# Batch 0's keys and queries: three adjacent tokens a partition in two halves, instead of two tokens a partition in three blocks

## The chip, the cores and the metric

The kernel runs on one core of a Trainium2 chip. A core has five engines with queues of their own (TensorE for matmuls, VectorE, ScalarE, GpSimd, and SyncE, which here issues most of the DMAs) and 16 DMA engines, which move data between the chip's memory and the core's on-chip buffers. Matmul results go into PSUM, in banks of 512 fp32 columns on 128 partitions; all else lies in SBUF. The metric is the time of one execution on the device, in microseconds (us), as the median of several runs.

## What is computed

Attention over 4 batches, 8 heads, 768 tokens and 64 numbers a head, with a window of fewer than 16 tokens to either side, and beside it one summary for each block of 32 tokens (the maximum of its keys, the mean of its values). Then a Fourier mix over tokens and channels, a normalization and two dense layers. Cut to what matters:

```python
k_sum = k.reshape(B, H, nb, 32, D).max(axis=3)
v_sum = v.reshape(B, H, nb, 32, D).mean(axis=3)
scores_l = scale * q @ k.T                      # kept where |i - j| < 16
scores_s = scale * q @ k_sum.T + log(32)
a = softmax(concatenate([scores_l, scores_s]))
x = a @ concatenate([v, v_sum])                 # then heads side by side: (B, 768, 512)
u = x + real(fft(fft(x, axis=1), axis=2))
out = u + maximum(layernorm(u) @ w_ch1, 0) @ w_ch2
```

All arithmetic is fp32; the weights come as float64 and are converted on the chip.

## The kernel before

Heads are taken in pairs: a group `g` holds heads 2g and 2g + 1, so a batch has four groups. Batch 0 is computed first and alone, by `first_attention`. For VectorE and TensorE its instructions stand in the order in which they are written (`tc.manual_schedule`), and SP issues the DMAs of that part in written order too (`fetch` pins them). For the rest the order on each engine is chosen when the program is built. The attention of the later batches is spread between the dense layers of the batch before.

For a group of batch 0 the steps are these.

- `load(b, g)` fetches the keys (`kn`) and the queries (`qn`), 384 KB each, into tiles with the tag `nat`, of which there are four. A partition p holds, for each of two heads `e` and of three blocks `j` of 256 tokens, the tokens 256 j + 2 p and 256 j + 2 p + 1. They lie next to each other in memory, so each run of bytes is 2 x 64 x 4 = 512 bytes.
- `prepare(b, g)` turns them so that the 64 numbers of a head lie along the partitions (two heads fill 128) and the tokens along the columns. It does so with matmuls against the identity: the loaded data are the stationary operand, `ident` the moving one. As a partition has every second token of its block, TensorE writes the columns `s`, `s + 2`, `s + 4`, ... of the bank (L700). The two heads go to the two halves of the partitions. ScalarE copies the banks to `kt` (keys, with 16 columns of padding at either end) or to `qt` (queries): one bank of 512 columns and one of 256 (L702). Then VectorE takes the maximum of each block of 32 keys into `km` (L715).
- `wide_scores(b, g)` multiplies keys and queries in stretches of 64 queries against 96 keys (L731) and against the block maxima (L735), for one half of the tokens (384) and then for the other. The first half of the queries is all that the first half of the scores needs of `qt`. ScalarE takes exponentials (L737), VectorE applies the band (`wide`).
- `wide_values(b, g)` multiplies by the values in `vw` (L758) and divides (L762 and after it).

At the start of the program, SP issues the loads of the keys and queries of group 0, of the keys of group 1, of a batch's values for the block means (`words`, 768 KB in rows of 8192 bytes), of the queries of group 1, and of the values in bands (`vw`). ScalarE issues five small tables: `ident`, `wide` (twice: the band and the counts), `sel` and `half`. L1468 is a VectorE instruction that multiplies `half` by 32; the text has it behind the first attention, and on VectorE it stands ahead of the first `km`. A pair of matmuls on a small tile (`warm`, L1414) runs on TensorE before the first data are there.

In the trace each fp32 matmul leaves two records, so the 12 matmuls that turn one tensor count as x24.

Of the kernel before, what the change touches and what calls it, by code (L numbers as in the profile page):

```python
# [16 lines left out]
P = 128  # L17
# [473 lines left out]
def _main_program(ctx, tc, q, k, v, moe_w_ch1, moe_w_ch2, out):  # L491


    nc = tc.nc
    B, H, S, D = q.shape
# [10 lines left out]
    S2 = S // 2  # L506
    F2 = S // 4
    HT = NST // 2
# [17 lines left out]
    ident = cpool.tile([P, P], FP, name="ident")  # L526
# [24 lines left out]
    def fetch(out, in_):  # L551

        ins = nc.sync.dma_start(out=out, in_=in_)
        if in_order[0]:
            tc.keep_in_program_order(ins)

    def abank(shape, name):
        return psum.tile(shape, FP, tag="attn", bufs=4, name=name)

    def bank(shape, name):  # L560
        return psum.tile(shape, FP, tag="bank", bufs=4, name=name)
# [10 lines left out]
    nat, marks = {}, {}  # L572

    def load(b, g, *which):

        for n in which or (1, 0):
            t = nat[b, g, n] = apool.tile([P, 2, NST // 2, 2 * D], FP, tag="nat", bufs=4, name=f"{'qk'[n]}n_{b}_{g}")
            if (b, g) > (2, 0):
                t = nat[b, g, n] = t.rearrange("p e j n -> p (e j n)").rearrange("p (m c) -> p m c", c=32)
                for e in range(2):  # L580
                    for h in range(2):
                        r, o = D * e + 32 * h, (q, k)[n][b, 2 * g + e].offset + 32 * h
                        fetch(out=t[r:r + 32], in_=bass.AP((q, k)[n].tensor, o, [[D, 32], [32 * D, S // 32], [1, 32]]))
                continue
            fetch(out=t.rearrange("p e j n -> p (e j) n"),
                  in_=(q, k)[n][b, 2 * g:2 * g + 2].rearrange("e (j p s) d -> p (e j) (s d)", p=P, s=2))

# [55 lines left out]
    is_wide = lambda b: b == 0  # L643
# [39 lines left out]
    def prepare(b, g, *which):  # L683
        qn, kn = (nat[b, g, n] for n in range(2))
        kt, km = kt_bufs[g % 2], km_bufs[g % 2]
        qt = apool.tile([P, S], FP, tag="qt", name=f"qt_{b}_{g}") if 0 in (which or (0,)) else None
        for n in which or (1, 0):
            src, dst = (kn, kt[:, W:W + S]) if n else (qn, qt)
            if (b, g) > (2, 0):
                with tc.issue_after(marks["dense"]):  # L690
                    nc.vector.transpose(out=dst, in_=src.rearrange("p m c -> p (m c)"))
                continue
            if is_wide(b):
                for j0, j1 in ((0, 2), (2, 3)):
                    n = 2 * P * (j1 - j0)
                    ps = bank([P, n], f"qk_{b}_{g}_{j0}")
                    for j in range(j0, j1):
                        for s in range(2):
                            for e in range(2):
                                nc.tensor.matmul(ps[D * e:D * (e + 1), 2 * P * (j - j0) + s:2 * P * (j - j0 + 1):2],  # L700
                                                 src[:, e, j, D * s:D * (s + 1)], ident, start=True, stop=True)
                    nc.scalar.copy(out=dst[:, 2 * P * j0:2 * P * j1], in_=ps)  # L702
            else:
                for e in range(2):

                    ps = abank([P, S2], f"qk_{b}_{g}_{e}")
                    for j in range(NST // 2):
                        nc.tensor.transpose(ps[:, P * j:P * (j + 1)], src[:, e, j, :], ident)
                    for s in range(2):
                        nc.scalar.copy(out=dst[D * e:D * (e + 1), s:S:2], in_=ps[D * s:D * (s + 1)])  # L710
        if which == (0,):
            nat[b, g] = qt
            return
        with tc.issue_after(marks["fold", 0]) if (b, g) == (1, 0) else ExitStack():
            nc.vector.tensor_reduce(out=km[:, 0:nb], in_=kt[:, W:W + S].rearrange("p (n f) -> p n f", f=BLOCK),  # L715
                                    op=ALU.max, axis=AX.X)
        nat[b, g] = qt
# [110 lines left out]
    def first_attention():  # L828
# [3 lines left out]
        wt["fold"] = split_fold(0, fold)  # L832
        p = {0: wide_scores(0, 0, lambda: add_blocks(0))}
        prepare(0, 1)
        sum_values(0, 0)
        load(0, 3)
        for g in range(NP - 1):
            p[g + 1] = wide_scores(0, g + 1, (lambda: add_blocks(1)) if g == 1 else None)
            wide_values(0, g, p[g], x)
            load_values(*following(0, g, 2))  # L840
            for par in range(2):
                fold_sequence(par, g)
            if g == 0:
                get_tables(0)
            if g < NP - 2:
                prepare(0, g + 2)
                sum_values(0, g + 1)
            if g == NP - 3:
                load_raw(1)
                load(1, 0)  # L850
                load_raw(2)
                sum_values(0, g + 2)
# [105 lines left out]
    def gen_attention(b):  # L958
# [3 lines left out]
        if b == 2:  # L962
            load(2, 1)
            load(2, 2)
# [4 lines left out]
        for g in range(NP + 1):  # L969
# [36 lines left out]
            if n1:  # L1006
                prepare(*n1, *((1,) if b > 1 else ()))
# [404 lines left out]
    ps = bank([P, 512], "warm")  # L1412
# [19 lines left out]
    for vw in vw_bufs:  # L1432
        nc.gpsimd.tensor_copy(out=vw[:, :, D].rearrange("p (e n) -> p e n", e=2),
                              in_=count[:, None, :].to_broadcast([P, 2, NQ]))
# [47 lines left out]
    for b in range(B):  # L1482
# [14 lines left out]
        if b == B - 2:  # L1497
# [9 lines left out]
            ps = bank([1, 1], "flag_ps")  # L1507
# [42 lines left out]
```

## Time and profile before

| | us |
|---|---|
| median of 3 runs | 804.05 |
| lowest and highest of them | 803.28, 805.3 |
| profiled execution | 800.91 |
| its span, first to last instruction | 799.1 |
| TensorE busy in the span | 775.9 |
| VectorE, ScalarE busy | 496.6, 224.5 |

The profiled execution is one execution with the hardware profiler on; its span leaves out 1.8 us around the first and last instruction. The granted clock of TensorE was 0.993 of full speed over the span, and 0.66 between 10 and 20 us. In that stretch TensorE worked 7.25 us of 10; in the one before it 8.00.

How to read the profile: a busy engine isn't always at its peak, since matmuls overlap. A row of the timeline gives the start, the length, the engine, the line, the operation, what it writes and reads, and in brackets how long the engine had been idle before it and what it waited for. A name as `sc<-qt,kt` is output and inputs. DMA engines were busy to 86% over the first 10 us and over 100% in the next 20 (their packets overlap).

### The profile page before, as it was taken

To read this page: it belongs to the slowest core of one execution; us is meant where nothing else is said; L and a number is where in the kernel's file an instruction comes from. 1 tells how busy PE (TensorE), PEld (TensorE's weight loads), DVE (VectorE), ACT (ScalarE), POOL (GpSimd) and SP (SyncE) were. 2 spreads that over 40 slices of the span, in tenths; PEclk is the share of its full clock that TensorE was granted. 3 is DMA by queue.
4 is the path that set the end of the run, shared out by engine and by line. 5 is a ranking of instruction groups with operands and counts; after the bars stand their busy time and mean duration, and the time that the engine had idled before them with its cause. 6 is when DMAs were issued, how large, how long until landed. Compare 5 with 4: busy or idle time off the path is not lost.

```text
span 799.1 us, 14452 instructions
## 1 busy us (share of the span) xinstructions
PE 775.9 (97%) x5914; PEld 566.1 (71%) x5914; DVE 496.6 (62%) x1131; ACT 224.5 (28%) x493; POOL 52.0 (7%) x91
## 2 busy tenths in 40 slices
PE   7979899999999999999999999999999999999997
PEld 4768665445589866688578876688569875786686
DVE  3798998985997647562668634554576622533352
ACT  2544866533735121100136012100126102001200
POOL 0010000000000320000210510000120000000000
PEclk8999999999999999999999999999999999999999
DMA  9999797978755469946343459501614153106001
GB/s 212 227 193 200 174 311 237 250 206 265 222 142 160 129 196 266 166 70 163 128 164 120 132 210 173 132 2 54 232 55 139 53 196 139 61 0 231 0 28 55
DMA packets 135258, 121.83 MB, mean 152 GB/s; under 512 B 94448, under 2 KB 116688, under 8 KB 134992
## 3 DMA queue, kind: packets, MB, share of 16 engines
q1 hardware_dynamic: 133920, 118.53, 54.0%
q0 software_dynamic: 576, 2.10, 0.8%
q8 instruction: 48, 0.79, 0.4%
q10 hardware_dynamic: 688, 0.20, 0.1%
q14 instruction: 26, 0.21, 0.1%
HBM read 97.22 MB, written 23.59 MB: 151 GB/s over the span
## 4 chain that ended last, share of the span: by engine, by line
PE 84%; DVE 12%; DMA 2%; issue 1%; ACT 1%; ACTq 0%; SPq 0%; DVEq 0%
PE hx L1307 19%; PE ox L1376 17%; PE hz L1307 9%; PE oz L1376 9%; PE o L1353 5%; PE hy L1307 5%; PE oy L1376 4%; PE y L1203 3%; PE mx L1162 2%; PE sc L774 2%; DVE x L566 2%; DMA half<-c_half 1%; PE av L812 1%; PE av L807 1%; DVE u L566 1%; DVE w L566 1%
## 5 line engine op out<-in xcount | busy, mean ns | idle before, releaser
L1307 PE MATMUL hx<-u,w 128*128 128x384 f32 x512 | 185.8, 490 | 0.3 <-DVE h L566 0.3
L1307 PEld LDWEIGHTS hx<-u,w 128*128 128x128 f32 x512 | 95.1, 190 | 67.5 <-ACT p L780 2.5
L1307 PE MATMUL hz<-u,w 128*128 128x384 f32 x256 | 93.1, 486 | 0.0
L1376 PE MATMUL ox<-w,s 128*128 128x256 f32 x336 | 80.3, 380 | 0.9 <-DVE x L566 0.9
L1376 PE MATMUL oz<-w,s 128*128 128x256 f32 x336 | 80.7, 379 | 0.0
L1376 PE MATMUL ox<-w,h 128*128 128x256 f32 x336 | 79.6, 381 | 0.0
L566 DVE TENSOR_TENSOR x<-ox,x 128x256 f32<-128x256 f32 x84 | 35.2, 422 | 65.2 <-PE ox L1376 64.9
L1307 PEld LDWEIGHTS hz<-u,w 128*128 128x128 f32 x256 | 48.6, 190 | 34.2 <-ACT h L1326 0.5
L1376 PEld LDWEIGHTS ox<-w,h 128*128 128x128 f32 x336 | 62.9, 190 | 11.2 <-issue 1.2
L1318 ACT COPY h<-hx 128x384 f32<-128x384 f32 x32 | 15.3, 479 | 195.7 <-PE hx L1307 195.7
L1376 PEld LDWEIGHTS ox<-w,s 128*128 128x128 f32 x336 | 63.1, 190 | 10.1 <-DVE x L566 1.6
L1376 PEld LDWEIGHTS oz<-w,s 128*128 128x128 f32 x336 | 63.5, 190 | 8.5
L566 DVE TENSOR_TENSOR h<-hx,h 128x384 f32<-128x384 f32 x32 | 17.8, 556 | 51.2 <-PE hx L1307 51.2
L566 DVE TENSOR_TENSOR h<-hy,h 128x384 f32<-128x384 f32 x32 | 17.8, 557 | 49.1 <-PE hy L1307 49.0
L1307 PE MATMUL hy<-u,w 128*128 128x384 f32 x128 | 46.6, 487 | 0.0
L1353 PE MATMUL o<-w,h 128*128 128x512 f32 x96 | 41.9, 594 | 0.0
L1337 ACT ACTIVATE h<-hx 128x384 f32<-128x384 f32 x32 | 15.7, 491 | 87.2 <-PE hx L1307 87.1
L1376 PE MATMUL oy<-w,h 128*128 128x256 f32 x168 | 39.9, 379 | 0.0
L566 DVE TENSOR_TENSOR x<-oz,x 128x256 f32<-128x256 f32 x42 | 17.8, 423 | 31.1 <-PE oz L1376 30.8
L1307 PEld LDWEIGHTS hy<-u,w 128*128 128x128 f32 x128 | 24.2, 190 | 16.6 <-DVE h L566 0.2
L1376 PEld LDWEIGHTS oy<-w,h 128*128 128x128 f32 x168 | 31.9, 190 | 4.3
L1353 PEld LDWEIGHTS o<-w,h 128*128 128x128 f32 x96 | 18.0, 190 | 22.3 <-issue 21.7
(164 smaller groups left out, 1091.2 us busy)
## 6 DMA issues: line engine op xcount, KB each, us to landing
w<-dw SPq DMA_DIRECT2D x44, 896.0 KB, 5.6
words<-in_moe_w_ch_dram SPq DMA_DIRECT2D x32, 512.0 KB, 5.9
dw<-w SPq DMA_DIRECT2D x12, 896.0 KB, 6.1
vw<-in_v_dram SPq DMA_DIRECT2D x47, 192.0 KB, 5.5
out_dram<-x SPq DMA_DIRECT2D x24, 256.0 KB, 2.3
vb<-in_v_dram SPq DMA_DIRECT2D x24, 192.0 KB, 3.6
kn<-in_k_dram SPq DMA_DIRECT2D x9, 384.0 KB, 5.8
qn<-in_q_dram SPq DMA_DIRECT2D x9, 384.0 KB, 6.6
```

Source lines behind the costliest of these rows:

```text
L566: return nc.vector.tensor_tensor(out=out, in0=in0, in1=in1, op=op).ins
L774: nc.tensor.matmul(ps[h][r:r + 64, i, :], kt[rows, o:o + 64], qt[rows, o:o + BLOCK], start=True, stop=True)
L807: nc.tensor.matmul(av[r][32 * j:32 * (j + 1), t, :], p[rows, h, i - NB2 * h, :], vw[rows, i, :], start=(t == 0), stop=False, skip_group_ch ...
L812: nc.tensor.matmul(av[r][:, t:t + HT + 1:HT, :], pm[rows, P * t:P * (t + 1)], vs[rows], start=False, stop=(t == HT - 1), skip_group_check= ...
L1162: nc.tensor.matmul(out, y[:, g], table, start=False, stop=True, skip_group_check=True)
L1203: nc.tensor.matmul(y, fgs[b][par][:, st, P * g:P * (g + 1)], fs[par][:, g % 2, st, :], start=(st == 0), stop=(st == n - 1))
L1307: ins = nc.tensor.matmul(ps, w[:, a, kk, :], u[:, r, kk, :], start=start and kk == 0, stop=stop and kk == 1, skip_group_check=True)
L1318: nc.scalar.copy(out=c11, in_=X)
L1337: nc.scalar.activation(out=c21, in_=X, func=AF.Relu)
L1353: nc.tensor.matmul(ps, h[:, n, hf, P * t:P * (t + 1)], wt[2, b, j][:, 2 * hf:2 * hf + 2, :], start=(n, hf) == (0, 0), stop=(n, hf) == (NC ...
L1376: nc.tensor.matmul(ps, left[a][:, n, :], wt[2, b, j][:, r, :], start=start and n == 0, stop=stop and n == NC - 1, skip_group_check=True)
```

## The change

For batch 0 alone, `load` makes another layout: a partition p holds, for each head and for each half `h` of 384 tokens, the three tokens 384 h + 3 p to 384 h + 3 p + 2. Each run of bytes is then 3 x 64 x 4 = 768 bytes, and a load has 2 x 2 x 128 = 512 of them where it had 2 x 3 x 128 = 768. The bytes, the number of DMAs and the tiles stay.

`prepare` follows it: for each half one bank of 384 columns, into which six matmuls write with a step of 3, and one copy of 384 columns to `kt` or `qt`. There are as many matmuls as before (12 for a tensor), with the same shapes, and as many copies (2).

```diff
             if is_wide(b):   # in load, new
+                t = nat[b, g, n] = t.rearrange("p e j n -> p (e j n)").rearrange("p (e h s d) -> p e h s d", e=2, h=2, s=HT)
+                fetch(out=t.rearrange("p e h s d -> p (e h) (s d)"),
+                      in_=(q, k)[n][b, 2 * g:2 * g + 2].rearrange("e (h p s) d -> p (e h) (s d)", p=P, s=HT))
+                continue
...
             if is_wide(b):   # in prepare
-                for j0, j1 in ((0, 2), (2, 3)):
-                    n = 2 * P * (j1 - j0)
-                    ps = bank([P, n], f"qk_{b}_{g}_{j0}")
-                    for j in range(j0, j1):
-                        for s in range(2):
-                            for e in range(2):
-                                nc.tensor.matmul(ps[D * e:D * (e + 1), 2 * P * (j - j0) + s:2 * P * (j - j0 + 1):2],
-                                                 src[:, e, j, D * s:D * (s + 1)], ident, start=True, stop=True)
-                    nc.scalar.copy(out=dst[:, 2 * P * j0:2 * P * j1], in_=ps)
+                for h in range(2):
+                    ps = bank([P, S2], f"qk_{b}_{g}_{h}")
+                    for s in range(HT):
+                        for e in range(2):
+                            nc.tensor.matmul(ps[D * e:D * (e + 1), s:S2:HT], src[:, e, h, s, :], ident, start=True, stop=True)
+                    nc.scalar.copy(out=dst[:, S2 * h:S2 * (h + 1)], in_=ps)
```

Here `P` is 128, `D` 64, `S2` 384 and `HT` 3; `src` is the loaded tile and `dst` the turned one.

More of the change, by code (lines that the diff above doesn't have):

```diff
@@ L584, in load @@
                 continue
+            if is_wide(b):
+                t = nat[b, g, n] = t.rearrange("p e j n -> p (e j n)").rearrange("p (e h s d) -> p e h s d", e=2, h=2, s=HT)
+                fetch(out=t.rearrange("p e h s d -> p (e h) (s d)"),
+                      in_=(q, k)[n][b, 2 * g:2 * g + 2].rearrange("e (h p s) d -> p (e h) (s d)", p=P, s=HT))
+                continue
             fetch(out=t.rearrange("p e j n -> p (e j) n"),
```

## The prediction

> **What bounds the kernel now.** I read the page first, then the chain of waits and the timeline of the first 55 us, because everything that the change touches happens there: the four head pairs of batch 0 are loaded and turned in the first 40 us.
>
> ```profile
> span 799.1 us, 14452 instructions
> PE 775.9 (97%) x5914; PEld 566.1 (71%) x5914; DVE 496.6 (62%) x1131; ACT 224.5 (28%) x493; POOL 52.0 (7%) x91
> PE   7979899999999999999999999999999999999997
> ```
>
> TensorE is the bound over the whole run; it has 23 us without work, and much of that lies in the first slices. The chain of waits for the first 75 us says which wait ends last there (start, length, what):
>
> ```profile
> 2.60 8.96 DMA half<-c_half
> 11.56 0.03 issue
> ...
> 11.67 0.10 DVE vs L1468
> 11.76 0.94 DVE km L715
> 12.70 0.04 issue
> 12.75 1.49 PE sc L735 x4
> ```
>
> The start hangs on a table of 1 KB. `half` is issued by ScalarE at 2.60 and lands at 11.56. VectorE has a small multiplication by it (L1468) ahead of the block maxima `km` (L715), TensorE needs `km` for L735, and so the keys and queries, ready long before, wait. The timeline shows the same engines:
>
> ```profile
> 5.13 1.75 PE L700 MATMUL qk<-ident,kn 128*64 128x128 f32 x24
> 6.49 0.86 ACT L702 COPY kt<-qk 128x512 f32<-128x512 f32 x2 [2.12 <-PE qk L700]
> 6.71 1.48 PE L700 MATMUL qk<-ident,qn 128*64 128x128 f32 x24
> 7.80 0.86 ACT L702 COPY qt<-qk 128x512 f32<-128x512 f32 x2 [0.45 <-PE qk L700]
> 8.44 1.24 PE L731 MATMUL sc<-qt,kt 64*96 64x64 f32 x24 [0.25 <-ACT qt L702]
> 11.67 0.17 DVE L1468 TENSOR_SCALAR vs<-half 128x2 f32<-128x2 f32 x1 [9.49 <-DMA half<-c_half]
> 11.74 0.95 DVE L715 TENSOR_REDUCE km<-kt 128x24 f32<-128x768 f32 x1
> 12.75 1.49 PE L735 MATMUL sc<-qt,km 64*32 64x384 f32 x4 [3.07 <-DVE km L715]
> ```
>
> TensorE has done its first scores by 9.68 and stands still for 3.07 us. The first loads themselves are not the wait: by the landings in the trace the keys are whole at 4.78 and the queries at 6.32; the warm-up matmuls hold TensorE until about 5.1, and the query transposes start at 6.71. From 12.75 to 32.76 the chain is nearly all TensorE, from 33.3 to 41.4 nearly all VectorE; in group 3 TensorE waits 0.64 us for `km` again (start 41.48).
>
> Why is `half` late? The trace's landings give one time for each of the 16 DMA engines: fifteen have their part of `half` between 7.13 and 8.70, the last at 11.56. In the packet records that last engine's share appears in steps of about 0.5 us among the 8192-byte packets of `words` (505 ns each), which follow the second key load in SP's queue.
>
> **What the Trainium skill says.** (1) "PSUM — Partial Sum Buffer", Specifications: cachelines of 8 bytes, and non-contiguous access slows matmuls significantly. The trace disagrees for fp32 with a step of 2: 24 matmuls in 1.48 us, the last lasting 0.27, run in pairs on both halves of the array, so a pair comes every (1.48 - 0.27) / 11 = 0.110 us; contiguous transposes with as many columns (L1281) follow each other every 0.109 us. With a step of 2 each element already has 8 bytes of its own, so with a step of 3 it touches no more lines. (2) "DMA: Bandwidth & Descriptors", Why small descriptors are slow: a packet carries about 3 cycles over its 32-byte beats. Estimate from that: 512 bytes are 16 + 3, 768 bytes 24 + 3; the trace has 28 ns for 512 bytes when nothing crowds it, so 768 bytes take 28 x 27/19 = 40 ns; half way between the trace's 28 ns and its 52 ns for 1024 bytes is 40 too. (3) The same page, Queues, rings and completion order: each DMA engine takes turns between queues, a packet at a time. The trace agrees: ScalarE's queue gets some 1 packet for 4 to 7 of the 512-byte ones, and 1 for 1 beside `words`.
>
> **The change, part by part.**
> - The loads. Each is 384 KB in 768 packets of 512 bytes, and will be 512 of 768 bytes: per DMA engine 48 x 28 = 1.34 us becomes 32 x 40 = 1.28 us, a gain of 0.06 us, up to 0.08 where the trace shows 35 ns. The gain lands on the path only at the start. There it moves the end of the three loads ahead of `words` by about 0.2 us, and `words` and the straggling part of `half` with it: -0.2 us. The fourth load of that time and the four later ones cost nothing and give nothing: groups 2 and 3 are issued at 14.26 and 24.85 and used at 27.5 and 36.0, and behind them in SP's queue stand loads of `vw` and `words` with room: `vw` of group 0 is down at 15.9 and read at 26.05. Were that cover gone, 0.08 us a load would be on the path, 0.3 us in all.
> - The matmuls. Before and after 12 instructions (24 matmul records) a tensor, with the same shapes; only the output's step goes from 2 to 3. By (1) their cost is taken as unchanged. Bounds: below, nothing, as 0.110 is already the contiguous pace; above, see the rival.
> - The copies. 587 + 378 ns for 512 and 256 columns become two of 384; the nearest rows, 384-column copies (L1318, 479 ns) and exponentials (484 to 491), say 2 x 480, the same sum. The order in time moves. The first copy now starts after 6 of 12 matmuls rather than 8: 2 pairs of passes sooner, 0.22 to 0.25 us, and is 0.1 us shorter, so the first 384 query columns, all that the first scores (L731) need, are there about 0.35 us sooner. The last copy is 0.1 us longer, so `km` can start 0.1 us later.
> - What that is worth by group. Group 0: scores start at 8.19 instead of 8.44, but the wait for `km` swallows it: 0. Group 1: the query copy ends at 20.90 + 0.59 = 21.49 and scores start at 21.55, 0.34 us after four matmuls that need 0.22: -0.1 us. `km` is done at 21.54 instead of 21.43 and read at 22.72: 0. Group 2: TensorE runs through (30.64): 0; `km` starts at 30.21 behind VectorE's own work: 0. Group 3: TensorE waits for VectorE, which is busy until 40.48: 0.
>
> Sum: -0.2 - 0.1 = -0.3 us. The profiled execution took 800.91 us (span 799.1 and 1.8 around it), below the three timed runs; on it this makes 800.6, on their median of 804.05 it makes 803.8.
>
> **The rivals.**
> - *The table slips further back.* ScalarE's queue has 38 packets per DMA engine up to `half`, and on fifteen engines it finished just as the second key load did (their last landings 8.25 and 8.70). If an engine counts packets when it takes turns, fewer packets ahead of `words` mean fewer turns for ScalarE before the slow part: some 6 to 8 packets would remain after `words`, each behind four packets of 40 ns: 7 x 0.16 = +1.1 us, so 805.1. At most `half` lands with the last of the second query load (13.28, +1.7), or, with those of `vw` too, near 15.9 (+4.3, beyond 2.4 if it lands after 14.0). For it: the close finish. Against: a row of a partition has 3072 bytes before and after, and if the turns go by rows nothing changes.
> - *The table gets through.* If the slow engine too finishes `half` ahead of `words`, it lands at about 8.7, `km` is ready at 9.7 and L735 follows the scores at 9.7: -3.0 us, 801.0. The same comes if the order of VectorE, which outside the hand-ordered part is chosen when the program is built, puts `km` ahead of L1468. For it: one engine of 16 decides. Against: that engine was 0.7 us behind with the keys too, and the change does little for ScalarE's queue.
> - *The step of 3 is slow*, the rival on the other side. Its elements start in turn at the first and the second half of an 8-byte line, where those of a step of 2 all start alike; no row here has such a step. Group 0 hides it in the 3 us of waiting, groups 1 to 3 hold 72 pairs, and 0.64 us of group 3 is slack. It exceeds 2.4 us when 72 x (p - 0.110) - 0.64 - 0.3 > 2.4, that is above p = 0.156 us a pair. At double the pace: 72 x 0.110 - 0.64 - 0.3 = +7.0 us, 811.0.
> - *It does not do what it says:* the runs are 768 bytes, but no wait that ends last is on them. That is nearly my forecast; pure nothing gives 804.05.
>
> **How the numbers follow.** What a measurement of this kernel tells from no change is about 0.3%, 2.4 us. My forecast (with nothing) has 0.62, the table slipping back 0.18, the table getting through 0.14, the slow step 0.06. Faster by over 2.4 us is the table getting through and little else: 0.16. Slower takes the slow step, the upper end of the slip, and a share for other orders that the builder may choose later in the program: 0.15. Same is the rest: 0.69. The likeliest case alone spans 803.0 to 804.6; the range goes from the table getting through (801.0, and 0.2 for the timing) to the slip beyond its middle: 800.8 to 806.0.
>
> **What would show it.** Right: L700 with pairs at 0.110 us, copies of 128x384, `half` landing at 11.3 to 11.5, L735 at about 12.5, packets fewer by 8 x 256 = 2048. Wrong: a pair above 0.12 us; `half` before 9 or after 12; `km` ahead of L1468; or a start as forecast and a total that differs by more than 1 us, when the cause would lie after 55 us.

## The result and the profile after

The first comparison had 16 executions of each kernel. The median was 802.81 us after (799.61 to 805.71) and 805.14 us before (803.28 to 808.27). The ratio after to before is **0.9975, with a 95% interval of 0.9957 to 0.9993**, which is -2.0 us (the medians themselves differ by 2.3, the means by 2.8). That is less than the 0.3% that I took as the least a measurement can tell from nothing. The interval still lies below 1, so it counts as a gain, and it is more than six times the forecast 0.3 us. Later comparisons made it smaller (below). The profiled execution of the changed kernel took 801.65 us, longer than the 800.91 of the one before. A single pair of executions says nothing at this size.

The page of the changed kernel, first its busy times, slices and packets (line numbers from `load` on are 2 to 5 higher than before: L700 is now L703, L731 L733, L735 L737, L758 L760, L708 L710):

```profile
span 799.7 us, 14452 instructions
PE 776.4 (97%) x5914; PEld 567.5 (71%) x5914; DVE 496.4 (62%) x1131; ACT 225.1 (28%) x493; POOL 52.2 (7%) x91
...
PE   8969899999999999999999999999999999999997
...
PEclk9969999999999999999999999999999999999999
...
DMA packets 133210, 121.83 MB, mean 152 GB/s; under 512 B 94448, under 2 KB 114640, under 8 KB 132944
```

TensorE has as many instructions and as much work as before. There are 135258 - 133210 = 2048 packets fewer, as forecast. Of the slices of 20 us, the first has gone from 7 to 8 (its clock from 8 to 9), the third, 40 to 60 us, from 7 to 6, and its granted clock from 9 to 6: something is better at the start and worse later.

The timeline of the start, after:

```profile
5.13 2.02 PE L703 MATMUL qk<-ident,kn 128*64 128x128 f32 x24
6.54 0.48 ACT L704 COPY kt<-qk 128x384 f32<-128x384 f32 x1 [2.02 <-PE qk L703]
...
6.98 1.48 PE L703 MATMUL qk<-ident,qn 128*64 128x128 f32 x24
...
8.39 1.24 PE L733 MATMUL sc<-qt,kt 64*96 64x64 f32 x24
...
8.89 0.17 DVE L1470 TENSOR_SCALAR vs<-half 128x2 f32<-128x2 f32 x1 [6.72 <-DMA half<-c_half]
8.97 0.94 DVE L717 TENSOR_REDUCE km<-kt 128x24 f32<-128x768 f32 x1
9.96 0.83 PE L737 MATMUL sc<-qt,km 64*32 64x384 f32 x4 [0.34 <-DVE km L717]
```

The 24 matmuls with a step of 3 take 1.48 us, as those with a step of 2 did: (1.48 - 0.27) / 11 = 0.110 us a pair. The copy shown is 0.48 us, and so is the second. In this execution `half` landed at 8.79 instead of 11.56, so TensorE waits 0.34 us for `km` and not 3.07. This looks like my rival "the table gets through", and it is worth 3 us at this point. But by the middle of the third slice little of it is left. The same timeline further on:

```profile
39.13 1.67 PE L760 MATMUL av<-vw,p 128*64 128x65 f32 x48
...
43.26 2.81 PE L760 MATMUL av<-vw,p 128*64 128x65 f32 x48 [2.46 <-DMA vw<-in_v_dram]
...
49.46 1.51 PE L710 MATMUL qk<-ident,kn 128*128 128x128 f32 x6 [3.38 <-DMA kn<-in_k_dram]
...
53.88 2.94 PE L1205 MATMUL y<-fs,fold 128*128 128x193 f32 x8
```

Before, the matching rows are

```profile
44.82 3.07 PE L758 MATMUL av<-vw,p 128*64 128x65 f32 x96
...
50.34 1.51 PE L708 MATMUL qk<-ident,kn 128*128 128x128 f32 x6 [2.45 <-DMA kn<-in_k_dram]
...
54.63 1.58 PE L1203 MATMUL y<-fs,fold 128*128 128x193 f32 x8
```

The kernel that started sooner reaches the last values of batch 0 sooner and finds them not yet loaded (2.46 us), and then waits longer for the keys of batch 1 (3.38 us against 2.45). Of the 3 us, 0.75 are left where the Fourier stage begins (`y<-fs`, 53.88 against 54.63). The chain of waits of the changed kernel goes back from there into SP's queue:

```profile
35.18 0.19 SPq L553
35.37 0.05 issue
35.42 7.70 DMA vw<-in_v_dram
43.12 0.14 issue
43.26 2.61 PE av L760 x46
```

And SP's own timeline, after, shows what stands in that queue (start, time spent issuing, what is loaded):

```profile
31.29 1.99 SPq L553 DMA_DIRECT2D fs<-c_fs  x2
33.32 0.43 SPq L553 DMA_DIRECT2D fd<-c_fd  x1
34.14 8.35 SPq L553 DMA_DIRECT2D vw<-in_v_dram  x6
42.58 0.39 SPq L553 DMA_DIRECT2D words<-in_moe_w_ch_dram  x1
43.02 0.50 SPq L553 DMA_DIRECT2D kn<-in_k_dram  x1
```

Issuing six transfers takes 8.35 us here, where one takes 0.4 when there is room: I read this as SP waiting for its queue, which is backlogged. (No wait for another engine that the profile shows is as long; that the queue is full is not itself in the trace.) Ahead of the last values of batch 0 stand the tables of the Fourier stage (`fs`, two of 579 KB, and `fd`, 768 KB), and the keys of batch 1 can only be issued behind all this.

The backlog isn't there all the way. In the profile of before, SP also stood for TensorE to free the buffers of the values (who waited for whom: us in total, times, longest):

```profile
SPq L553 <- PE av L758: 4.0, 3, 1.9
```

Between 33 and 34 us, between two of these waits, the DMA engines were busy to 0.03 only. The two runs of the changed layout in which `half` is late (below) have waits of this kind too, of 1.1 to 2.5 us at 24 to 36 us. Time saved on a load can't be handed on in full across them.

So there were two theories for the 2 us. **Table:** the layout lets `half` through sooner. **Queue:** the layout shortens the packets, and what that saves is handed down SP's backlog to the waits at 43 to 50 us. A third, **neither**, says that the comparison was luck.

### The profile page after: what moved, and what is told of

Read it like the earlier page. It is cut to its first block, busy times and chain, and to the rows that moved or that the text cites. A ratio compares the mean times of both kernels' runs of the same rounds, so it can differ in the third digit from the quotient of the medians.

```text
span 799.7 us, 14452 instructions
## 1 busy us (share of the span) xinstructions
PE 776.4 (97%) x5914; PEld 567.5 (71%) x5914; DVE 496.4 (62%) x1131; ACT 225.1 (28%) x493; POOL 52.2 (7%) x91
## 2 busy tenths in 40 slices
DMA packets 133210, 121.83 MB, mean 152 GB/s; under 512 B 94448, under 2 KB 114640, under 8 KB 132944
## 4 chain that ended last, share of the span: by engine, by line
PE 84%; DVE 11%; DMA 2%; issue 1%; ACT 1%; ACTq 0%; SPq 0%; DVEq 0%
PE hx L1309 19%; PE ox L1378 17%; PE hz L1309 9%; PE oz L1378 9%; PE o L1355 5%; PE hy L1309 5%; PE oy L1378 4%; PE y L1205 4%; PE mx L1164 2%; PE sc L776 2%; DMA vw<-in_v_dram 1%; DVE x L566 1%; PE av L814 1%; PE av L809 1%; DVE u L566 1%; DVE w L566 1%
```

## The experiments

Every ratio below is to the kernel before, run in the same series on the same chip (medians 803.33, 803.99 and 803.87 us in the three series, with 59, 43 and 52 executions).

**Both kernels again.** No edit. The table theory needs `half` early in every execution of the one and late in the other.

> The kernel before, unchanged, for a second profile of its start. Theory 1 (the late table): `half` lands after 11 us because one DMA engine has its packets among those of `words`; if that is how the kernel is and not chance, it lands at 11 to 12 again, L735 starts at 12.3 to 13.2, and a stretch at half clock begins before 20 us. Theory 2 (chance): the landing moves between 8.5 and 12 from one execution to the next, and the 2 us between the kernels have another cause. Ratio 1.000 by both.

> The changed kernel, unchanged, for a second profile. Theory 1: `half` lands before 9.2 again, L737 (L735 before) starts at about 10, no half clock before 40 us, ratio 0.9975 with about 0.002 to either side. Theory 2 (chance): `half` lands anywhere from 8.5 to 12.

Measured: before 803.85 us, ratio 1.0011 (0.9994 to 1.0028); after 803.00, ratio 0.999 (0.9965 to 1.0014). In this execution of the kernel before, `half` landed at 9.42, early too, and its waits are those of the changed kernel (engine, what it waits for: us in total, times, longest):

```profile
PE av L758 <- DMA vw<-in_v_dram: 3.3, 1, 3.3
PE qk L708 <- DMA kn<-in_k_dram: 2.9, 1, 2.9
```

The wait for `vw` therefore comes without the change too, with an early start, and an early `half` isn't the change's doing.

**The multiplication by `half` later.** In both kernels (L1468 before, L1470 after):

```diff
-    nc.vector.tensor_scalar(out=vs[:, :, D], in0=half_of, scalar1=float(BLOCK), scalar2=None, op0=ALU.mult)
+    tc.keep_in_program_order(nc.vector.tensor_scalar(out=vs[:, :, D], in0=half_of, scalar1=float(BLOCK), scalar2=None, op0=ALU.mult))
```

> The kernel before, with the VectorE instruction that reads `half` (L1468) kept behind the first attention, so that `km` waits for the keys alone. Theory 1 (all of the gain is the wait for the table): `km` at about 7.4, L735 at 9.7, and as fast as the changed kernel or up to 1 us faster: ratio 0.996 to 0.998. Theory 2 (the gain comes from the loads' fewer packets, or from the copies' order): the start moves by 3 us and the total stays, ratio 0.999 to 1.001.

> The changed kernel with L1470 (L1468 before) kept behind the first attention in the same way. Theory 1: the table was no longer late, so this gives 0.3 us at the start (TensorE's 0.34 us of waiting for `km`) and nothing that can be measured in total: ratio 0.996 to 0.998, within 0.001 of the kernel before with the same edit. Theory 2 (packets or copies): 0.002 to 0.003 better than the kernel before with the same edit.

Measured: 803.27 us, 0.9999 (0.9985 to 1.0013), and 803.31, 1.0006 (0.9993 to 1.002). The edit didn't do what it was for. It keeps the multiplication only behind the memset of `vs` one line above, and that one still goes to the front of VectorE's order; the profile has the multiplication where it was, waiting 7.0 us for `half`. They count as repeats of the two kernels. As such they have a use: in the changed one `half` landed at 10.98, late, and yet its profiled execution (span 798.1 us) is the shortest of the five of the changed layout in the table below.

**Pinned behind the first attention.** Now both lines are kept in order, so that nobody waits for `half` at the start:

```diff
-    nc.vector.memset(vs, 0.0)
-    nc.vector.tensor_scalar(out=vs[:, :, D], in0=half_of, scalar1=float(BLOCK), scalar2=None, op0=ALU.mult)
+    tc.keep_in_program_order(nc.vector.memset(vs, 0.0))
+    tc.keep_in_program_order(nc.vector.tensor_scalar(out=vs[:, :, D], in0=half_of, scalar1=float(BLOCK), scalar2=None, op0=ALU.mult))
```

> The kernel before, with both VectorE instructions on `vs` (L1467, L1468) kept behind the first attention: the edit of the run before_late left L1468 where it was. No execution can wait for `half` now, so the start is the early one each time (L735 at about 9.7). Theory A (absorbed): what the start gains is waited for later, at the last group's values and at the keys of batch 1, both DMAs, so the total stays: ratio 0.999 to 1.001, and the profile shows 2 us or more of TensorE waiting for `vw` and for `kn` between 40 and 50 us. Theory B (the start counts): 2 to 3 us off those executions in which the table is late, 0.997 to 0.999.

> The changed kernel with the same two instructions behind the first attention. With the run before_pin it shows the change without the table's chance. Theory A (fewer packets relieve the queue behind which `vw` and `kn` of batch 1 stand): 0.5 to 1.5 us below the kernel before with the same edit, ratio 0.998 to 0.999. Theory B (the change acts on the table alone): the two are equal within 0.3 us.

Measured: before with it 803.65 us, 0.9994 (0.9974 to 1.0013); after with it 802.60, 0.9984 (0.9969 to 0.9998). In the kernel before `half` landed at 11.33 and held nobody up. The pin gained nothing that can be measured. That alone is weak evidence: `half` was late in only one of the three unpinned profiles of the kernel before so far, so the pin could have given about 1 us on average, and the interval allows 2; and in the profiled execution the first queries landed at 8.51 instead of 6.32, so that TensorE waited 2.11 us for them. Between the two pinned kernels, where `half` plays no part at all, there is 803.65 - 802.60 = 1.05 us in favour of the change (0.6 by means, with 1.6 either way), which is not clear of noise. That an earlier start is absorbed is seen better in the table below.

**One token a partition.** The changed kernel with packets of 256 bytes and a step of 1: the opposite direction for the queue, with the start and TensorE's work kept.

```diff
-                fetch(out=t.rearrange("p e h s d -> p (e h) (s d)"),
-                      in_=(q, k)[n][b, 2 * g:2 * g + 2].rearrange("e (h p s) d -> p (e h) (s d)", p=P, s=HT))
+                fetch(out=t.rearrange("p e h s d -> p (e h s) d"),
+                      in_=(q, k)[n][b, 2 * g:2 * g + 2].rearrange("e (m p) d -> p (e m) d", p=P))
...
-                            nc.tensor.matmul(ps[D * e:D * (e + 1), s:S2:HT], src[:, e, h, s, :], ident, start=True, stop=True)
+                            nc.tensor.matmul(ps[D * e:D * (e + 1), P * s:P * (s + 1)], src[:, e, h, s, :], ident, start=True, stop=True)
```

> The changed kernel with one token a partition and block of 128 (1536 runs of 256 bytes a load instead of 512 of 768), the banks written without a step. Copies and their order as in the changed kernel. Theory A (packets of the loads matter): the loads take 96 packets of 20 to 30 ns a DMA engine, 2.4 us against 1.28; query data of group 0 land 1.5 to 2 us later, the start and the values of the last group too, ratio 1.001 to 1.004. Theory B (the packets are hidden): ratio within 0.001 of the changed kernel. If a step of 3 costs TensorE anything, pairs here come faster than 0.110 us.

Measured: 806.64 us, 1.0041 (1.0026 to 1.0055). This is the slowest kernel of the study, though its `half` landed earliest of all, at 7.79. Its waits, in the profile:

```profile
PE av L760 <- DMA vw<-in_v_dram: 4.7, 1, 4.7
PE qk L710 <- DMA kn<-in_k_dram: 1.9, 1, 1.9
PE qk L703 <- DMA kn<-in_k_dram: 1.9, 2, 1.6
```

The wait for `vw` has grown to 4.7 us, and batch 0's own keys are now waited for too. Its transposes, with a step of 1, are no faster:

```profile
5.53 1.53 PE L703 MATMUL qk<-ident,kn 128*64 128x128 f32 x24 [0.33 <-DMA kn<-in_k_dram]
```

That is (1.53 - 0.27) / 11 = 0.115 us a pair, against 0.110 with steps of 2 and 3.

**The Fourier tables later.** If the backlog ahead of `vw` and the batch 1 keys decides, taking 1.9 MB out of its way should give more than the change did, in either layout:

```diff
-            if g == 0:
-                get_tables(0)
...
             if g == NP - 3:
                 load_raw(1)
                 load(1, 0)
                 load_raw(2)
+                get_tables(0)
```

> The changed kernel with the three Fourier tables (1.9 MB) issued behind the values of group 3 and the keys and queries of batch 1, instead of ahead of them. Theory A (the start's gain is lost to those DMAs): the waits for `vw` and `kn` of 2.1 to 3.4 us each go, the first Fourier matmul (53.9 us in the profile after) comes 2 to 4 us earlier, less time at half clock follows, ratio 0.994 to 0.997. Theory B (VectorE's folds set the Fourier's start anyway): under 1 us, ratio 0.999 or more.

> The kernel before with the Fourier tables issued behind the values of group 3 and the keys and queries of batch 1, as in the run after_tab. Theory A (in the kernel before and in the changed one the end of batch 0's DMAs decides): the move alone gives most of the gain of after_tab, ratio 0.9965 to 0.998, and the change on top of it is worth less than without it, as the late DMAs are off the path: within 0.5 us of after_tab. Theory B (the change acts earlier, at the start): after_tab stays 1 us or more below this run.

Measured: after with it 801.04 us, 0.9966 (0.9949 to 0.9983); before with it 802.32, 0.9983 (0.9961 to 1.0006). The first is a gain; the interval of the second reaches past 1, so for the layout before it isn't shown. In both profiles the wait for `vw` is gone (96 matmuls in one piece), and after has only this left of the waits for loads:

```profile
PE qk L710 <- DMA kn<-in_k_dram: 1.3, 1, 1.3
```

SP issues the keys of batch 1 at 38.03 (after) and 40.19 (before). TensorE's first Fourier matmul `y<-fs` starts at 49.38 and 51.41, in both kernels sooner than in any profile with the tables in their old place (52.12 at the earliest). The 2 us between the two can't all be put down to the change: in this execution of before the first queries landed at 7.77, and TensorE waited 1.9 us for queries.

**Keys of batch 1 first, tables last; and the pin with the tables moved.** The best order I had. In the first, `load(1, 0)` goes where `get_tables(0)` was:

```diff
             if g == 0:
-                get_tables(0)
+                load(1, 0)
...
                 load_raw(1)
-                load(1, 0)
                 load_raw(2)
+                get_tables(0)
```

> The run after_tab with the keys and queries of batch 1's first group issued one group earlier still, ahead of the values of group 3. The wait of 1.3 us for `kn` in that run's profile should go; the values of group 3 come up to 2.5 us later, for which that run has no wait. If DMAs still set the Fourier's start, 0.5 to 1.5 us below after_tab, ratio 0.995 to 0.9965; if VectorE sets it (theory B), equal to it.

> The run after_tab with the two instructions on `vs` behind the first attention as in after_pin. With the tables out of the way a start that never waits for `half` should now reach the end: in the profiles of the changed kernel the table was late (10.98) once in three and cost about 3 us then, so 0 to 1 us below after_tab on the median, ratio 0.9945 to 0.9965. If the start is absorbed elsewhere (theory A of before_pin), equal to after_tab.

Measured: 799.54 us, **0.9934 (0.9911 to 0.9958)**, and 799.55, 0.9951 (0.9936 to 0.9967). Both beat the kernel before, and the changed kernel in the same series (`after_third`, below): by 3.8 us (1.4 either way) and 2.75 us (0.9) on the means. In the timeline of the first:

```profile
40.19 3.07 PE L760 MATMUL av<-vw,p 128*64 128x65 f32 x96
...
43.19 0.88 PE L710 MATMUL qk<-ident,kn 128*128 128x128 f32 x6
...
46.16 0.84 PE L710 MATMUL qk<-ident,qn 128*128 128x128 f32 x6 [2.10 <-issue]
```

No wait for a load is left there; the keys' transposes follow the last values at once. What is late next is 2.10 us that the profile puts down to no releaser. In the second I expected the pin to be of use at last, with no `vw` to eat the sooner start. Its ratio is lower than that of the tables alone (0.9951 against 0.9966), but the intervals overlap, and in neither of the two does `y<-fs` start sooner than with the tables alone (49.45 and 49.96 against 49.38). What they gain beyond it, if it is more than chance, lies elsewhere and is not followed here.

**The changed kernel a third time.** No edit, on another chip.

> The changed kernel once more, for its size. Theory A (fewer packets): the eight loads' packets take 10.8 to 11.4 us a DMA engine where the kernel before has 12.3 to 13.0, SP comes to the keys of batch 1 at 42.4 to 44.5 (before 44.4 to 46.9), and the total is 0.5 to 2 us lower: ratio 0.9975 to 0.9995. Theory B (the first comparison was chance): ratio 0.9995 to 1.001.

Measured: 802.51 us, 0.9982 (0.9969 to 0.9995). `half` landed at 10.85.

**The table and the queue side by side.** From the trace of each profiled execution of the two layouts, pinned ones included (`half`: when its last part landed; packets: the time that those of the eight key and query loads of batch 0 took, for one DMA engine of 16; keys: when SP issues the keys of batch 1; `y`: start of the first `y<-fs`; all in us):

| kernel | `half` | packets | keys | `y` |
|---|---|---|---|---|
| before | 11.56 | 12.25 | 44.36 | 54.63 |
| before, again | 9.42 | 12.98 | 44.91 | 55.11 |
| before, edit without effect | 9.03 | 12.86 | 44.66 | 54.92 |
| before, pinned | 11.33 | 12.38 | 46.89 | 57.18 |
| after | 8.79 | 11.35 | 43.02 | 53.88 |
| after, again | 9.07 | 11.27 | 44.13 | 54.57 |
| after, edit without effect | 10.98 | 10.86 | 42.43 | 52.12 |
| after, pinned | 9.71 | 10.82 | 44.47 | 55.02 |
| after, third | 10.85 | 11.23 | 42.75 | 53.06 |
| one token | 7.79 | about 16.7 | 46.36 | 56.52 |

(The packets of one token are an estimate: its loads have 256 bytes a packet, as those of `vw` have. The two together took 28.7, and the packets of `vw` took 11.4 to 12.6 in the traces of the other two layouts, 12 in the middle.)

`half` lands early and late in both layouts: it varies from one execution to the next, and **the table theory falls**. Nor does an early `half` bring an early `y`: before it comes at 54.63 with `half` at 11.56, and at 55.11 and 54.92 with `half` at 9.42 and 9.03; after, the two late ones have 52.12 and 53.06, the early ones 53.88 and 54.57. So the sooner start is absorbed. The packets part the layouts without overlap: 12.6 us on average before, 11.1 after, 1.5 less. The other two columns overlap a little from one execution to the next (the pinned kernels are later in both layouts), but within each pair of kernels the change is ahead, and on average keys are issued 1.8 us sooner (45.2 to 43.4) and `y` starts 1.7 us sooner (55.5 to 53.7). Without the pinned pair, whose kernel before had its queries late, it is 1.6 and 1.5 us. So about as much comes out at the end of the queue as the 1.5 us that the packets save. That is the queue theory, and two other runs go with it: one token (packets up, time up, with the copies of the changed kernel) and the changed kernel with the tables moved (backlog shorter, time down). One token also shows that it isn't one for one: some 5.6 us more of packets than after move the keys by 3.0 us and `y` by 2.8. How far the equality of 1.5 and 1.5 to 1.8 is chance stays open.

**How large is it?** The differences of the means of single executions are -2.8 us (95% bounds 1.1 either way) in the first comparison, -0.5 (0.8) in the second, where the repeats count on each side, and -1.1 (0.75) in the third. The second alone doesn't tell a gain from nothing; the other two do. They spread by more than these bounds allow, so something differs from series to series that their intervals don't hold. Weighed together they give about -1.2 us, and I would trust it no further than "about 1 us, between 0.5 and 3".

## Why the prediction was right, and where it was not

- **Forecast and range.** 803.8 us on a median of 804.05 was -0.3 us. Measured -2.0 in the first comparison and about -1.2 over all, inside the range, and the likeliest class (within 0.3%) holds. The size was off by a factor of about 4 over all. That the class held is in part luck: -0.2 of the sum lay where the gain isn't found, and the gain came by a path that I had put at nothing.
- **The step of 3 costs nothing**: right. 0.110 us a pair, as forecast; this rival falls. The Trainium skill's "PSUM — Partial Sum Buffer", Specifications, has non-contiguous access slow matmuls significantly; for steps of 1, 2 and 3 in fp32 these runs have 0.115, 0.110 and 0.110, so the measurement decides against it here.
- **Copies, packets, VectorE's order**: right. 0.48 us each, 2048 packets fewer, `km` still behind the multiplication. Of the earlier first copy one thing can be seen: TensorE waits 0.25 us for it ahead of the first scores in all five profiles of the old layout, and in none of the nine of the new ones.
- **"`words` and the straggling part of `half` with it: -0.2 us"**: this step fails. `half` was named the wait that the start hangs on, from one execution. It landed anywhere from 9.03 to 11.56 in the same kernel before; 0.2 us can't be seen beside that. And the start isn't worth what it seemed: a `half` that lands 2 us sooner brings no earlier `y`.
- **"The fourth load of that time and the four later ones cost nothing and give nothing"**: this is the step that failed in earnest. I counted the cover only up to the next tile in the queue, `vw` of group 0, which has 8 to 10 us of room (the forecast has it down at 15.9; its last part landed at 17.54, and it is read at 26.05). But SP's queue is backlogged for much of the first 50 us, and time saved on a load can be handed from one transfer to the next until it reaches one that TensorE waits for: the last `vw` of batch 0 and the keys of batch 1. The keys are issued 1.6 to 1.8 us sooner on average. The profile of before had this end in TensorE's waits (`kn`, 2.4 us), and I didn't follow the queue that far.
- **The saving in a load**: mis-sized. I had put 40 ns for a packet of 768 bytes, an estimate from the Trainium skill's "DMA: Bandwidth & Descriptors", Why small descriptors are slow, and 0.06 to 0.08 us a load. The median packet of 512 bytes took 27 ns before, near my 28, and that of 768 bytes 36 after (means in this crowded stretch 33 and 43). Over eight loads it is 1.5 us, 0.19 a load. "Were that cover gone ... 0.3 us in all" was the right sentence with the wrong number: at 0.19 a load the five later loads give about 0.95 us, and all eight 1.5.
- **The table gets through**: it did, in the first profile of the changed kernel, and it would have been an easy story: `half` early, result near 801. The runs say that it was chance, that the kernel before has it too (2 of its 3 unpinned profiles with the tables in place, and 2 of 4 after), and that nearly all of the 3 us is lost again by 54 us. **The table slips back** doesn't happen through the change either, for the same reason.
- **What would show it wrong**, "`half` before 9", was met in the first execution. And the total differed by more than 1 us with a cause, as far as it was found, before 55 us; I had looked for it after 55.

A reading that doesn't hold throughout: that the queues take turns a packet at a time. Beside `words` it is 1 for 1, but beside the 512-byte packets one for 4 to 7 (about one for 3 between 6 and 7 us), so the unit of a turn stays open.

Not settled: the part of the gain that comes from the first three loads rather than the later five (no kernel changed one group alone); the part of the copies (no kernel changed the loads and kept the old copies, though one token shows that the packets alone can move the total); how the saved time passes SP's waits for TensorE where `half` is late; and why the three comparisons differ.

## What to carry to other kernels

When a queue is backlogged, follow a saved microsecond down the queue to the transfer that somebody waits for, not to the next one; a cover ends only where the queue runs empty or its issuer waits for something else. A wait that ends last in one execution must be seen in a second one before a forecast is built on it, above all if it hangs on a small transfer between large ones. And look at what stands in the queue ahead of the late transfer: within one series, changing the place of 2.7 MB of tables and keys took the changed kernel from 0.18% to 0.66% below the one before, and the reshaping of 3 MB of loads is the first 0.18%.

## What the runs showed of the hardware

- Pauses of TensorE are followed by a lower granted clock, so here they cost twice. The table of stretches of the changed kernel (stretch and its length; busy us and instructions of PE, PEld, DVE, ACT and POOL; granted clock, DMA share, GB/s):

```profile
40.00:50.00 10.00, 4.16 (x78) 3.88 (x75) 8.12 (x21) 0.11 (x1) 1.31 (x5) 0.69 0.87 213
50.00:60.00 10.00, 8.95 (x40) 8.11 (x39) 6.46 (x16) 5.33 (x13) 2.26 (x3) 0.63 1.10 196
```

In the clock records it is at half from 43.71 to 57.4, 13.65 us, which begins 0.45 us after the wait for `vw` ended. Where TensorE stood 3 us at the start, a stretch of half clock lay there (12.4 to 19.3 before) and the one at 50 us was shorter. All have lengths in multiples of 3.41 us (3.41, 6.83, 10.24, 13.65), except the last of each execution, which its end cuts off. I read this as one way in which an earlier start is paid back. The Trainium skill's "TensorE: Matmul & The Clock Gate", Part 1, has the clock go to half after an idle window of about 3.4 us; these stretches agree with that length, but a wait need not fill a whole window. In the first 100 us of the fourteen profiles 28 stretches at half clock begin, each behind 3.41 us in which TensorE stood for 1.26 to 3.41 us (2.46 in this one), and only once for all of it; pieces of 3.41 us in which it stood for up to 1.81 us were not followed by one. In `y<-fs` the same eight matmuls take 2.94 us at half clock and 1.58 at full.
- The time of an execution goes with its mean granted clock. Over the 16 executions of the changed kernel the correlation is -0.83, from 805.71 us at 0.985 to 799.61 at 0.997. It varies: over 59 executions of the kernel before it is -0.70, over the 22 of the changed kernel in the third comparison only -0.14. With a scatter of some 6 us, a change of 1 us needs tens of executions on each side.
